# Attention with a feed-forward layer on one core: the products' moving columns are read from two halves in turn

## The chip, the core and the metric

The kernel runs on one core of a Trainium2 chip. The metric is the device time of one execution in microseconds (us). Before the change it was 906.98 us, the median of three runs that lay between 906.57 and 907.24 us.

## What is computed

The reference computes attention and, on its output, a feed-forward layer. Attention has 8 batches, 8 heads, 576 tokens and a head size of 64; it is causal, each token sees the 128 newest tokens, and a slope per head is added to the scores:

```
scores = scale * q @ k.T ; bias by distance ; keep 0 <= rel < 128 ; softmax ; @ v
x   = attention output as (4608 tokens, 512)
h   = max(x @ w_in, 0)            # w_in: 512 x 2048
out = (h * h) @ w_out             # w_out: 2048 x 512
```

All of it is float32. The tokens are independent of one another in the feed-forward layer, so their order inside a block of columns is free as long as the output is put back.

## The kernel before, in words

The 4608 tokens are nine chunks of 512. Activations lie with features on the 128 partitions and tokens along the free dimension, so in every product of the feed-forward layer the weights are stationary (128 by 128) and the tokens are the moving columns. The output is written transposed (512 features by 4608 tokens), and the host turns it back with `.T` at the end of `kernel` (line 1542).

**Float32r in three products.** TensorE's float32r type keeps fewer bits than float32. Each operand is therefore split into a high part and a low part, and a block is the sum of three products: high by high, low weight by high, high weight by low. Every such product is one weight load and one matmul.

**Four places issue float32r products.** `gemm1` (line 244) is the first layer for chunks 0 and 1: 12 matmuls of 512 columns for each of the 16 feature blocks f of a chunk. `product` (line 344) is the first layer for chunks 2 to 8; there a pair of feature blocks, two halves of the reduction and two halves of the chunk's tokens make a 2 by 2 problem that is done in seven products, not eight, each of six matmuls of 256 columns (7 chunks x 8 pairs x 7 x 6 = 2352). `part` (line 518) is the second layer for chunks 0 to 7: 16 f x 4 blocks x 3 matmuls of 512 columns a chunk. `third` (line 432) is the second layer of the last chunk, again in seven products: 8 pairs x 2 x 7 x 3 = 336 matmuls of 256 columns. The attention products (lines 601, 650, 714, 873, 886, 918) and the transposes (955, 958) are plain float32 and small.

**Where the weights lie.** Converted weights are kept as `w[f]` with shape `[128, 2, 512, 2]`: the last index is low or high part, so `block` (line 227) hands out weights in which one column lies two words behind the last. For a quarter of the first layer's feature blocks (`APART`, line 41: f = 0, 4, 8, 12, blocks 0 and 1) two columns' pairs are laid alternately, so there one column lies four words behind the last. For the seven products, `operand` (line 307) hands out pieces 0, 3 and 5 of the tile `flow` with a step of two words and the other four with neighbouring columns. In `third`, M1, M2 and M4 take `w` with a step of two words, the rest the tile `second` with neighbouring columns.

**Moving operands.** `x[c, p]` (tile `xu`, shape `[128, 2, 512]`), `tees`, `hh`, `hl`, `h2`, `keep` and `turned` all hold a product's 256 or 512 columns as neighbouring words; each matmul reads them from first to last.

**Order of the work.** A planner (`Plan.run`) takes steps with written costs, due times and hand-tuned nudges, simulates the queues and issues the instructions in the order that it finds; that order is fixed when the program is built. The planner's costs of PE steps (such as 0.7 for a block of `part`) are numbers in the code. From chunk 2 on, a visit of about 4 us with attention work comes between the products every 24 us.

## Time and profile before

| | |
|---|---|
| median of three runs | 906.98 us (906.57 to 907.24) |
| the profiled execution | its time is given by its span alone, 905.9 us from the first to the last instruction |
| instructions | 23570 |
| matmuls on PE | 8700, each with its own weight load |
| granted TensorE clock | 1.000 over the whole span |

The profile shows one execution. Engines: PE is TensorE's matmul, PEld its weight load, DVE is VectorE, ACT is ScalarE, POOL is GpSimd, SP issues DMAs. Matmuls are pipelined: a matmul's listed duration reaches well into the next one, so the pace is read from one start to the next, or from the chain of work, whose pieces follow one another without overlap.

### The profile page before, as it was taken

To read this page: it belongs to the slowest core of one execution; us is meant where nothing else is said; L and a number is where in the kernel's file an instruction comes from. 1 tells how busy PE (TensorE), PEld (TensorE's weight loads), DVE (VectorE), ACT (ScalarE), POOL (GpSimd) and SP (SyncE) were. 2 spreads that over 40 slices of the span, in tenths; PEclk is the share of its full clock that TensorE was granted. 3 is DMA by queue.
4 is the path that set the end of the run, shared out by engine and by line. 5 is a ranking of instruction groups with operands and counts; after the bars stand their busy time and mean duration, and the time that the engine had idled before them with its cause. 6 is when DMAs were issued, how large, how long until landed. Compare 5 with 4: busy or idle time off the path is not lost.

```text
span 905.9 us, 23570 instructions
## 1 busy us (share of the span) xinstructions
PE 899.1 (99%) x8700; PEld 807.1 (89%) x8700; DVE 629.8 (70%) x1695; ACT 482.0 (53%) x1361; POOL 319.4 (35%) x403
## 2 busy tenths in 40 slices
PE   9999999999999999999999999999999999999998
PEld 6788888888899999999999999999999999989998
DVE  6998882677775677666766786676766565566675
ACT  7899663665654555444544555445545454444341
POOL 4222334665522333234333433233322222234341
DMA  9976326768888888788887788888887777669962
GB/s 347 404 279 213 88 62 200 244 225 265 300 273 285 286 269 261 261 281 271 284 270 265 259 269 272 294 265 273 267 301 241 232 238 225 209 204 341 301 226 94
DMA packets 142324, 229.77 MB, mean 254 GB/s; under 512 B 15744, under 2 KB 50176, under 8 KB 142208
## 3 DMA queue, kind: packets, MB, share of 16 engines
q1 hardware_dynamic: 141920, 227.87, 75.4%
q8 instruction: 68, 1.11, 0.5%
q10 hardware_dynamic: 288, 0.39, 0.1%
q14 instruction: 48, 0.39, 0.1%
HBM read 178.91 MB, written 49.28 MB: 252 GB/s over the span
## 4 chain that ended last, share of the span: by engine, by line
PE 95%; DMA 4%; ACT 0%; POOL 0%; issue 0%; DVE 0%; SPq 0%; POOLq 0%; DVEq 0%
PE acc L518 40%; PE chain L344 18%; PE rest L344 13%; PE g L244 10%; PE s L873 5%; PE acc L432 2%; PE g L886 2%; DMA raw<-in_dram 2%; PE s L432 1%; PE s L886 1%; DMA wide<-in_dram 1%; PE at L650 1%; DMA qk<-in_dram 1%; PE s L714 0%; PE chain L432 0%; PE rest L432 0%
## 5 line engine op out<-in xcount | busy, mean ns | idle before, releaser
L518 PE MATMUL acc<-hh,w 128*128 128x512 f32 x1024 | 361.8, 398 | 0.0
L518 PEld LDWEIGHTS acc<-hh,w 128*128 128x128 f32 x1024 | 200.4, 196 | 35.9 <-issue 5.5
L518 PE MATMUL acc<-hl,w 128*128 128x512 f32 x512 | 202.2, 395 | 0.0
L638 POOL TENSOR_SCALAR_AFFINE_SELECT pp<-pp 128x512 f32<-128x512 f32 x128 | 99.3, 785 | 169.2 <-DMA pp<-way 122.6
L571 POOL TENSOR_TENSOR t<-t,nm 128x512 f32<-128x512 f32 x64 | 67.8, 1062 | 250.4 <-DVE nm L567 191.9
L344 PEld LDWEIGHTS rest<-xu,flow 128*128 128x128 f32 x1008 | 142.5, 191 | 11.7
L344 PE MATMUL chain<-tees,flow 128*128 128x256 f32 x1008 | 147.4, 282 | 0.0
L344 PE MATMUL rest<-xu,flow 128*128 128x256 f32 x1008 | 146.8, 281 | 0.0
L364 ACT COPY four<-chain 128x256 f32<-128x256 f32 x56 | 20.9, 374 | 233.6 <-PE chain L344 233.6
L349 DVE TENSOR_TENSOR four<-four,rest 128x256 f32<-128x256 f32 x112 | 47.2, 421 | 124.8 <-PE rest L344 122.1
L344 PEld LDWEIGHTS chain<-tees,flow 128*128 128x128 f32 x1008 | 132.2, 191 | 0.0
L518 PEld LDWEIGHTS acc<-hl,w 128*128 128x128 f32 x512 | 100.3, 196 | 11.1
L559 ACT ACTIVATE t<-t,nm 128x128 f32<-128x128 f32 x256 | 100.3, 394 | 8.8 <-DVE nm L552 8.2
L244 PE MATMUL g<-xu,w 128*128 128x512 f32 x384 | 95.2, 396 | 0.0
L244 PEld LDWEIGHTS g<-xu,w 128*128 128x128 f32 x384 | 76.5, 209 | 12.8 <-issue 0.3
L552 DVE CUSTOM_DVE_ANT_0 t<-t,cst 128x128 f32<-128x128 f32 x256 | 62.8, 300 | 1.7
L262 DVE TENSOR_TENSOR hl<-r,hh 128x512 fp32r<-128x512 f32 x32 | 29.2, 913 | 45.0 <-ACT hh L260 45.0
L873 PE MATMUL s<-pp,v 64*64 64x128 f32 (+1 forms) x1792 | 52.3, 248 | 0.2
L344 PEld LDWEIGHTS chain<-xu,flow 128*128 128x128 f32 x336 | 48.2, 196 | 4.1 <-ACT four L364 0.5
L786 DVE COPY_PREDICATED t<-cst,s 64x256 f32<-64x256 int32 x100 | 44.4, 444 | 8.1 <-PE s L873 4.5
L344 PE MATMUL chain<-xu,flow 128*128 128x256 f32 x336 | 49.7, 284 | 0.0
L559 ACT ACTIVATION_READ_ACCUMULATOR t<-t,nm 128x1 f32 x256 | 48.3, 189 | 0.0
(159 smaller groups left out, 1378.0 us busy)
## 6 DMA issues: line engine op xcount, KB each, us to landing
flow<-ws SPq DMA_DIRECT2D x392, 256.0 KB, 5.1
raw<-in_dram SPq DMA_DIRECT2D x32, 512.0 KB, 8.8
way<-pp SPq DMA_DIRECT2D x256, 64.0 KB, 2.3
pp<-way SPq DMA_DIRECT2D x64, 256.0 KB, 2.7
qk<-in_dram SPq DMA_DIRECT2D x32, 320.0 KB, 5.7
v<-in_dram SPq DMA_DIRECT2D x32, 320.0 KB, 5.7
qk<-in_dram SPq DMA_DIRECT2D x38, 256.0 KB, 5.5
out_dram<-o SPq DMA_DIRECT2D x34, 256.0 KB, 3.2
```

What stands on the lines that cost most here:

```text
L244: nc.tensor.matmul(g, w, xs[cc][:, part], start=i == 0, stop=i == 11)
L262: nc.vector.tensor_tensor(hl, r, hh.bitcast(F32), op=ALU.subtract)
L344: self.latest = self.nc.tensor.matmul(to, w, x, start=start and k == 0, stop=k == 5, skip_group_check=True)
L349: add = lambda to, x: nc.vector.tensor_tensor(to, to, x, op=ALU.add)
L432: self.nc.tensor.matmul(self.total[u][name], w, x, start=j == k == 0 and name in ("M1", "M3", "M5", "M2"), stop=j == NF // 2 - 1 and k == ...
L518: self.latest = self.nc.tensor.matmul(self.acc[m], w, h, start=(f == 0 and i == 0), stop=(f == NF - 1 and i == 2))
L552: self.nc.vector.tensor_tensor_reduce(self.t[:, m], self.t[:, m], self.K.nrel(2 * self.p + m // 2), -0.125, BIG, ALU.add, ALU.min, self.nm ...
L559: return self.nc.scalar.activation(self.t[:, m], self.t[:, m], AF.Exp, bias=nm[:, 4 + m : 5 + m], scale=-1.0, accum_out=nm[:, m : m + 1],)
L571: self.nc.gpsimd.tensor_tensor(*(x.rearrange("p (j i) c -> p j i c", j=2) for x in (self.t, self.t)), self.rec.unsqueeze(3).to_broadcast([ ...
L638: nc.gpsimd.affine_select(to, self.own, pattern=[[-32 * sign, 4], [0, 4], [-sign, 32]], compare_op=op, fill=0.0, base=0, channel_multiplie ...
L786: nc.vector.copy_predicated(d, mask.unsqueeze(1).to_broadcast([64, 2, 2, 64]), e)
L873: yield self.nc.tensor.matmul(to, w, x, start=first and n < 2, stop=not first, skip_group_check=True)
```

## The change

Each of the four places that issue float32r products reads its moving columns through a helper, `turns`. It leaves the tile where it is and reads columns 0, h, 1, h+1, 2, h+2 and so on, where h is half the number of columns (256 of 512, or 128 of 256). The product's output is still written to neighbouring words, so the tokens of a chunk come out in another order. Both layers turn the order once. For chunks 0 and 1 both turn the whole chunk; for chunks 2 to 7 the first layer turns each half of 256 columns and the second the whole; for chunk 8 both turn each half. The host undoes this by indexing the columns of the output before it transposes it. No other instruction, tile, DMA, planner cost or due time is edited.

```
+def turns(x):
+    return x.rearrange("p (h c) -> p c h", h=2)

 gemm1:
-                nc.tensor.matmul(g, w, xs[cc][:, part], start=i == 0, stop=i == 11)
+                nc.tensor.matmul(g, w, turns(xs[cc][:, part]), start=i == 0, stop=i == 11)
 product:
-            self.latest = self.nc.tensor.matmul(to, w, x, start=start and k == 0, stop=k == 5, skip_group_check=True)
+            self.latest = self.nc.tensor.matmul(to, w, turns(x), start=start and k == 0, stop=k == 5, skip_group_check=True)
 third:
-                self.total[u][name], w, x, start=...
+                self.total[u][name], w, turns(x), start=...
 part:
-            self.latest = self.nc.tensor.matmul(self.acc[m], w, h, start=(f == 0 and i == 0), stop=(f == NF - 1 and i == 2))
+            self.latest = self.nc.tensor.matmul(self.acc[m], w, turns(h), start=(f == 0 and i == 0), stop=(f == NF - 1 and i == 2))

+def _order():
+    turn = lambda n: np.arange(n).reshape(2, n // 2).T.reshape(-1)
+    whole, half = turn(512), np.concatenate([turn(256), 256 + turn(256)])
+    at = np.empty(B * S, int)
+    for c in range(NCH):
+        one, two = whole if c < 2 else half, half if c == NCH - 1 else whole
+        at[512 * c + one[two]] = 512 * c + np.arange(512)
+    return at

 kernel:
-    return np.ascontiguousarray(r.results[0]["out_0_dram"].T)
+    return np.ascontiguousarray(r.results[0]["out_0_dram"][:, _order()].T)
```

## Rows read from the trace of the kernel before

**Rows 1.** The page, part 1: busy time, share of the span and instructions of each engine.
```profile
PE 899.1 (99%) x8700; PEld 807.1 (89%) x8700; DVE 629.8 (70%) x1695; ACT 482.0 (53%) x1361; POOL 319.4 (35%) x403
```

**Rows 2.** The chain that ended last, shares of the span by line.
```profile
by line: PE acc L518 40.0%; PE chain L344 17.7%; PE rest L344 13.1%; PE g L244 9.6%; PE s L873 4.8%; PE acc L432 2.5%; PE g L886 2.4%; DMA raw<-in_dram 2.0%; PE s L432 1.3%; PE s L886 1.2%; DMA wide<-in_dram 1.0%; PE at L650 0.8%; DMA qk<-i
```

**Rows 3.** Waits: all of PE's, PEld's longest, then other engines': us, times, longest.
```profile
PE g L173 <- DVE zero L166: 1.3, 1, 1.3
PE acc L601 <- DVE xu L614: 1.1, 3, 0.6
PE s L714 <- ACT raw L215: 0.8, 1, 0.8
...
PEld acc L518 <- issue: 5.5, 32, 0.2
...
ACT four L364 <- PE chain L344: 233.6, 56, 5.3
...
DVE four L349 <- PE rest L344: 122.1, 100, 5.0
```

**Rows 4.** Chain pieces in order of time: start us, length us, engine, tile, line, matmuls.
```profile
48.49 2.80 PE g L244 x12
51.29 2.80 PE acc L518 x12
...
118.22 2.80 PE g L244 x12
121.02 2.80 PE acc L518 x12
...
174.45 2.76 PE g L244 x12
```

**Rows 5.** Busy time by windows: window, us, engines (instructions), clock, DMA share, GB/s.
```profile
50.00:100.00 50.00, 50.00 (x353) 42.12 (x352) 44.00 (x97) 44.42 (x91) 13.53 (x20) 1.00 0.58 196
100.00:150.00 50.00, 50.00 (x305) 41.86 (x305) 34.33 (x76) 27.70 (x66) 18.90 (x23) 1.00 0.32 87
400.00:450.00 50.00, 50.00 (x548) 45.63 (x550) 37.08 (x105) 25.60 (x77) 18.60 (x25) 1.00 0.85 284
```

**Rows 6.** Timeline of PE, five bf16 warming matmuls of 768 columns in all, and the next.
```profile
27.71 0.50 PE L173 MATMUL g<-zero 128*128 128x128 bf16 x5
28.04 0.28 PE L955 MATMUL at<-cst,tw 128*128 128x128 f32 x1
```

**Rows 7.** Timeline of PE around 411 us (start us, us): two products and the next.
```profile
411.14 0.88 PE L344 MATMUL rest<-xu,flow 128*128 128x256 f32 x6
411.86 0.88 PE L344 MATMUL chain<-tees,flow 128*128 128x256 f32 x6
412.57 0.40 PE L518 MATMUL acc<-hh,w 128*128 128x512 f32 x1
```

**Rows 8.** Groups of matmuls and of small weight loads by form: busy us, mean ns.
```profile
L518 PE MATMUL acc<-hh,w 128*128 128x512 f32 x1024 | 361.8, 398 | 0.0
L518 PE MATMUL acc<-hl,w 128*128 128x512 f32 x512 | 202.2, 395 | 0.0
L244 PE MATMUL g<-xu,w 128*128 128x512 f32 x384 | 95.2, 396 | 0.0
...
L873 PEld LDWEIGHTS s<-pp,v 64*64 64x64 f32 x1792 | 40.7, 134 | 5.1 <-issue 1.1 <-POOLq L890 0.4 <-POOL both L291 0.4
```

**Rows 9.** Weight loads of single lines: duration ns min/median/max; the last 59.3 to 60.5 us.
```profile
L432 PEld LDWEIGHTS s<-xu,second x72: 186/188/193, 835.7 to 896.7; 128*128 128x128 f32 x72
L432 PEld LDWEIGHTS acc<-xu,w x48: 193/197/203, 840.6 to 899.2; 128*128 128x128 f32 x48
...
L244 PEld LDWEIGHTS g<-xu,w x6: 308/310/311, 59.3 to 60.5; 128*128 128x128 f32 x6
```

**Rows 10.** Timeline of PE, first and seventh matmul of feature block 4 in `gemm1`.
```profile
59.53 2.72 PE L244 MATMUL g<-xu,w 128*128 128x512 f32 x11
...
60.94 1.31 PE L244 MATMUL g<-xu,w 128*128 128x512 f32 x5
```

**Rows 11.** Timeline of PE after a visit: the first two matmuls of line 518.
```profile
403.97 0.51 PE L518 MATMUL acc<-hh,w 128*128 128x512 f32 x1
404.31 0.40 PE L518 MATMUL acc<-hl,w 128*128 128x512 f32 x1
```

## The prediction

> **What bounds the kernel now.** I read the busy shares first. PE is busy for 899.1 of 905.9 us, while DVE stands at 70% [rows 1]. A busy PE can still be one that is held up inside, so the chain of work came next: the float32r lines 518, 344 and 244 alone are 80.4% of the span, and line 432 adds 3.8% [rows 2]. The waits say that nobody feeds PE late: its three waits sum to 3.2 us, while ACT and DVE wait for PE by the hundred microseconds [rows 3]. So the time is the number of float32r matmuls times their pace, and a change in that pace comes out in the total almost one for one.

> The pace: twelve matmuls of 512 columns take 2.80 us, 233.3 ns each, or 2.76 us, 230 ns each, in one stretch [rows 4]. For 256 columns the chain gives 17.7% + 13.1% of 905.9 us = 279.0 us over 2352 matmuls, 118.6 ns each [rows 2]; six in a row take 0.71 to 0.72 us, the same [rows 7]. [...]

> **The change part by part.** It removes no instruction and adds none; the order on each queue is the planner's, whose costs are untouched, and the DMAs are the same. The host's indexing is outside the device's time. What changes is the address of each moving column. With the halves taken in turn, the even columns are the neighbouring words of the first half, the odd ones those of the second. No row of this trace shows a product read in that way, so I bound it.

> Products of 512 columns: 1024 + 512 + 384 = 1920 [rows 8]. The chain gives them (40.0% + 9.6%) of 905.9 us, 449.3 us or 234.0 ns each [rows 2]. In 32 places [rows 3] the first one after a visit takes 340 ns, some 107 more than the others [rows 11]; that is 3.4 us which stay, so the pace in the stream is 232.2 ns. With two readers at 0.84 ns for their own column the stream would run at 0.42 a column: 512 x 0.42 + 3.9 = 219 ns; the bf16 row gives 215.5. I take 217 and a gain of 15.2 ns: 29.2 us. Of these, 2 x 4 x 6 = 48 in line 244 have loads with a step of four words, and there the loads set the pace already: six matmuls in 60.94 − 59.53 = 1.41 us, 235 ns, beside 310 − 80 = 230 ns of reading [rows 9, 10]. They gain nothing, which takes off 0.7 us. Sum 28.5 us; bounds 25 (219) and 31 (215.5).

> Products of 256 columns: 2352 + 336 = 2688. By columns alone they would fall from 118.6 to 256 x 0.42 + 3.9 = 111.4. But the next load must be read meanwhile, and the row above says pace = reading + 5 ns where the load is longer. Neighbouring weights: 108 + 5 = 113 ns. Weights with a step of two words: 117 + 5 = 122, more than they take now, so I give those nothing. Four of seven products have neighbouring weights, 1344 + 192 = 1536: (118.6 − 113) x 1536 = 8.6 us. Bounds: 0, if the loads already set the pace of all, and 9.9 x 2688 = 26.6 us, if they set none (108.7).

> [...]

> What is late next: in the window from 50 to 100 us ACT is busy for 44.4 and DVE for 44.0 of 50 us [rows 5], so a PE that is 6% faster there would meet weights and hidden blocks that aren't ready. The cover is thin for that window alone; I take 1 us back, with 0 and 3 us (the window's whole gain) as ends. In the later windows DVE has a quarter of its time free and the DMA share of 0.85 would rise to about 0.88.

> Sum: −28.5 − 8.6 + 1 = −36 us, 4% of 905.9. The median of the runs lies 1.1 us above the profiled span, and the same is assumed after: 907 − 36 = 871 us.

> **The rivals.** (1) *Slower: one group held at a time.* If both columns of a step come out of one fetch by one reader, then after the change each column needs a fetch of its own. The loads show what this does: from a step of two words to four, a column doubles. It decides from the point where two columns in a row lie in different groups, which is every column here. A column of a product would go from 0.448 to 0.896: +229 ns for 512 columns, +115 for 256, 1920 x 0.229 + 2688 x 0.115 = 749 us, a time of about 1656 us. At the 1.80 of a whole fetch for each column it would be 3170. For it speaks the load row at 310 ns, the only strided one of that kind; against it, that a product's two columns cost what a load's step of two costs. [...] (2) *No change.* If two groups are held at once but by one fetcher, there are as many fetches as before, 128 for 512 columns, and the pace stays: 907 us. [...] (3) *All of it.* If the weights with a step of two words don't hold their products either, the bounds are reached: 907 − 31 − 26.6 = 849 us. (4) *Less of it.* If the loads already set the pace of all products of 256 columns, 907 − 28.5 + 1 = 880.

> **How the numbers follow.** Two readers, gain as summed, 871 us: 0.45. All of it, 849: 0.14. Less of it, 880: 0.14. No change, 907: 0.07. One group at a time, 1656 or more: 0.20. About 0.2% (1.8 us) is what a measurement of this kernel can tell from no change. So faster 0.73, same 0.07, slower 0.20. The range goes from just under 849 to 909 and takes in every case but the slow one: 847 to 909. The forecast's own range is 860 to 882.

> **What would show it.** In the chain, pieces of twelve on lines 518 and 244 should fall from 2.80 to about 2.60 us, while the first six of line 244 at a step of four words stay at 235 ns each. On line 344 products with neighbouring weights should take 0.68 us for six, the others 0.72. Loads should keep their durations. PE should still be busy for 98% or more, with a few waits for ACT or DVE before 100 us. The forecast is wrong if pieces of twelve are at 5.5 us or more (one group at a time), or still at 2.80, or if the 256-column products gain as much a column as the long ones.

## The result, and the profile after the change

The kernel after the change takes 884.7 us (median of four runs, 883.4 to 886.12) beside 906.84 us (906.57 to 907.24) before: a ratio of 0.9754, interval 0.9739 to 0.9768. The forecast was 871 us. The gain has the forecast's sign, but is 22.1 us where 36 were forecast. The profiled execution took 883.4 us with a span of 881.7 us, 24.2 us less than the span before. Lines behind the new helper stand five lower now, so that 244, 344, 432 and 518 are 249, 349, 437 and 523, and `convert`'s 215 to 223 are 220 to 228.

The busy shares of the kernel after, in the form of [rows 1]:

```profile
PE 863.8 (98%) x8700; PEld 801.0 (91%) x8700; DVE 643.3 (73%) x1695; ACT 488.1 (55%) x1361; POOL 329.2 (37%) x403
```

PE lost 35.3 us of busy time, nearly as many as the forecast wanted from the whole. But DVE gained 13.5 us and ACT 6.1, though their instructions are the same. The chain by engine, first before and then after the change, and the chain of the kernel after by line, against [rows 2]:

```profile
PE 95%; DMA 4%; ACT 0%; POOL 0%; issue 0%; DVE 0%; SPq 0%; POOLq 0%; DVEq 0%
```

```profile
PE 74%; DMA 13%; DVE 6%; issue 2%; ACT 2%; POOL 1%; SPq 1%; DVEq 0%; POOLq 0%; ACTq 0%
PE acc L523 30%; PE chain L349 16%; PE rest L349 12%; PE s L878 5%; PE g L249 4%; DMA flow<-ws 3%; DMA raw<-in_dram 3%; PE acc L437 2%; PE g L891 2%; DMA pp<-way 2%; DVE w L228 2%; DVE raw L224 1%; DMA way<-pp 1%; POOL pp L643 1%; PE s L437 1%
```

The chain now runs outside PE for a quarter of the span, where before it was on PE for 95%. Its pieces in order of time show the first long stretch of this (start, length, work), against [rows 4]:

```profile
85.54 1.55 ACT raw L220
...
97.44 1.54 DVE raw L224
99.00 1.63 ACT w L226
100.66 1.64 DVE w L228
102.91 1.56 DVE raw L224
...
144.30 3.00 PE g L249 x12
147.30 2.59 PE acc L523 x12
149.89 2.59 PE g L249 x12
152.48 2.59 PE acc L523 x12
```

Between 41 and 141 us it runs for the most part over the conversion of weights (`convert`, lines 220 to 228), over other work of DVE and over DMAs; then over products again, of which twelve take 2.59 us, 215.8 ns each, not 2.80. Later it leaves PE again, mainly for DMAs, at 169, 286, 396 and 423 us. That the chain runs elsewhere doesn't say that PE stands still there; the windows do. They are, for the kernel after (columns as in [rows 5]):

```profile
50.00:100.00 50.00, 46.52 (x339) 39.59 (x339) 45.91 (x84) 48.13 (x85) 17.50 (x17) 1.00 0.58 193
100.00:150.00 50.00, 45.60 (x295) 39.69 (x294) 40.38 (x89) 31.68 (x76) 20.35 (x21) 1.00 0.27 71
400.00:450.00 50.00, 48.73 (x525) 45.84 (x524) 39.48 (x114) 27.08 (x86) 18.12 (x25) 1.00 0.85 293
```

PE was busy for all of each window before. Now 7.9 of the 100 us from 50 to 150 are idle, 3.5 of them before 100 us and 4.4 behind it, while ACT is at 48.1 of the first 50 us and DVE at 45.9. PE's longest waits between 45 and 166 us (who, for whom; us, times, longest), where it waited for nothing before the change:

```profile
PE at L655 <- POOL pp L643: 3.2, 4, 1.2
PE g L249 <- ACT r L258: 2.0, 4, 1.0
PE at L655 <- ACT t L772: 1.4, 1, 1.4
PE s L719 <- ACT r L263: 0.8, 1, 0.8
```

None of them is for a converted weight. They are for other instructions of ACT and POOL, which now come later. The conversions themselves, in the view of groups (busy us, mean ns, idle before), first before and then after:

```profile
L223 DVE TENSOR_TENSOR w<-raw,w 128x1024 fp32r<-128x1024 f32 x16 | 21.2, 1331 | 0.2
L219 DVE SCALAR_TENSOR_TENSOR raw<-raw 128x1024 int32<-128x1024 int32 x16 | 20.4, 1281 | 0.4
L215 ACT ACTIVATE raw<-raw 128x1024 f32<-128x1024 f32 x16 | 18.1, 1170 | 0.0
L221 ACT CAST w<-raw 128x1024 fp32r<-128x1024 f32 x13 | 14.8, 1144 | 0.3 <-DVE raw L219 0.2
```

```profile
L228 DVE TENSOR_TENSOR w<-raw,w 128x1024 fp32r<-128x1024 f32 x16 | 25.8, 1620 | 0.5 <-ACT w L226 0.3
L224 DVE SCALAR_TENSOR_TENSOR raw<-raw 128x1024 int32<-128x1024 int32 x16 | 25.5, 1606 | 0.4
L220 ACT ACTIVATE raw<-raw 128x1024 f32<-128x1024 f32 x16 | 22.4, 1473 | 0.0
L226 ACT CAST w<-raw 128x1024 fp32r<-128x1024 f32 x13 | 20.3, 1578 | 2.5 <-DVE raw L224 2.4
```

The same instructions on the same data take 22 to 38% longer, 19.5 us more over these four groups. (A fifth step of `convert`, DVE's shift in line 222, goes from 684 to 827 ns.) All of them read and write every second word (`raw` and `w` hold pairs), on engines that the change doesn't touch; the cast of `hh` from the neighbouring words of `r` is as before (622 ns, 620 before). So the first question for the experiments is whether the order in which PE reads can slow other engines, and the second whether the two readers are the right picture of the gain.

Products of 256 columns, the timeline of PE around 411 us after the change, against [rows 7] (start, us):

```profile
411.06 0.88 PE L349 MATMUL chain<-xu,flow 128*128 128x256 f32 x6
411.77 0.39 PE L523 MATMUL acc<-hh,w 128*128 128x512 f32 x1
...
413.08 0.83 PE L349 MATMUL rest<-xu,flow 128*128 128x256 f32 x6
413.75 0.83 PE L349 MATMUL chain<-tees,flow 128*128 128x256 f32 x6
414.42 0.39 PE L523 MATMUL acc<-hh,w 128*128 128x512 f32 x1
```

The first product has weights with a step of two words and takes 0.71 us for six as before; the other two have neighbouring weights and take 0.67 us, 112 ns each.

### The profile page after: what moved, and what is told of

It reads as the page before. It is cut to its first block, busy times and chain, and to the rows that moved or that the text cites. A ratio compares the mean times of both kernels' runs of the same rounds, so it can differ in the third digit from the quotient of the medians.

```text
span 881.7 us, 23570 instructions
## 1 busy us (share of the span) xinstructions
PE 863.8 (98%) x8700; PEld 801.0 (91%) x8700; DVE 643.3 (73%) x1695; ACT 488.1 (55%) x1361; POOL 329.2 (37%) x403
## 4 chain that ended last, share of the span: by engine, by line
PE 74%; DMA 13%; DVE 6%; issue 2%; ACT 2%; POOL 1%; SPq 1%; DVEq 0%; POOLq 0%; ACTq 0%
PE acc L523 30%; PE chain L349 16%; PE rest L349 12%; PE s L878 5%; PE g L249 4%; DMA flow<-ws 3%; DMA raw<-in_dram 3%; PE acc L437 2%; PE g L891 2%; DMA pp<-way 2%; DVE w L228 2%; DVE raw L224 1%; DMA way<-pp 1%; POOL pp L643 1%; PE s L437 1%
## 5 line engine op out<-in xcount | busy, mean ns | idle before, releaser
L523 PE MATMUL acc<-hh,w 128*128 128x512 f32 x1024 | 347.7, 384 | 0.0
L523 PE MATMUL acc<-hl,w 128*128 128x512 f32 x512 | 194.3, 379 | 0.1
L643 POOL TENSOR_SCALAR_AFFINE_SELECT pp<-pp 128x512 f32<-128x512 f32 x128 | 106.9, 843 | 178.8 <-DMA pp<-way 110.7
L349 PEld LDWEIGHTS rest<-xu,flow 128*128 128x128 f32 x1008 | 140.2, 194 | 6.8 <-DVE four L354 0.5
L349 PE MATMUL chain<-tees,flow 128*128 128x256 f32 x1008 | 142.7, 278 | 0.0
L349 PE MATMUL rest<-xu,flow 128*128 128x256 f32 x1008 | 142.3, 277 | 0.1
L349 PEld LDWEIGHTS chain<-tees,flow 128*128 128x128 f32 x1008 | 128.6, 194 | 0.0
L249 PE MATMUL g<-xu,w 128*128 128x512 f32 x384 | 90.8, 386 | 2.0 <-ACT r L258 2.0
L557 DVE CUSTOM_DVE_ANT_0 t<-t,cst 128x128 f32<-128x128 f32 x256 | 64.6, 309 | 1.7
L791 DVE COPY_PREDICATED t<-cst,s 64x256 f32<-64x256 int32 x100 | 44.4, 444 | 10.2 <-PE s L878 6.5
L267 DVE TENSOR_TENSOR hl<-r,hh 128x512 fp32r<-128x512 f32 x32 | 26.7, 835 | 31.4 <-ACT hh L265 31.3
```

Source lines behind the costliest of these rows:

```text
L249: nc.tensor.matmul(g, w, turns(xs[cc][:, part]), start=i == 0, stop=i == 11)
L267: nc.vector.tensor_tensor(hl, r, hh.bitcast(F32), op=ALU.subtract)
L349: self.latest = self.nc.tensor.matmul(to, w, turns(x), start=start and k == 0, stop=k == 5, skip_group_check=True)
L523: self.latest = self.nc.tensor.matmul(self.acc[m], w, turns(h), start=(f == 0 and i == 0), stop=(f == NF - 1 and i == 2))
L557: self.nc.vector.tensor_tensor_reduce(self.t[:, m], self.t[:, m], self.K.nrel(2 * self.p + m // 2), -0.125, BIG, ALU.add, ALU.min, self.nm ...
L643: nc.gpsimd.affine_select(to, self.own, pattern=[[-32 * sign, 4], [0, 4], [-sign, 32]], compare_op=op, fill=0.0, base=0, channel_multiplie ...
```

## The experiments

In all of them `turns` takes a second argument, a pattern, and each layer has a list with one pattern for each chunk (`ONE` for the first, `TWO` for the second); the host's order follows from the lists. "Partners" are two columns that are read one right after the other; in the change they lie 256 words apart (128 in a product of 256 columns).

```
+WAYS = {"plain": ("p c -> p c", {}),
+        "halves": ("p (h c) -> p c h", dict(h=2)),            # the change
+        "quarters": ("p (h c) -> p c h", dict(h=4)),
+        "pairs": ("p (h c b) -> p c h b", dict(h=2, b=2)),
+        "second": ("p (c h) -> p h c", dict(h=2)),            # every second column
+        "near16": ("p (b h c) -> p b c h", dict(h=2, c=16)),  # partners 16 words apart
+        ...
+def turns(x, way):
+    if way == "plain":
+        return x
+    pattern, sizes = WAYS[way]
+    return x.rearrange(pattern, **sizes)
```

### Chunk 0 as before, and chunk 0 with near partners

The conversions run beside chunk 0's products, so chunk 0 alone was edited, first back to plain reading, then to partners 16 words apart:

```
e1: ONE = ["plain"] + ["halves"] * 8;   TWO = ["plain"] + ["halves"] * 8
e3: ONE = ["near16"] + ["halves"] * 8;  TWO = ["near16"] + ["halves"] * 8
```

> Chunk 0 reads its columns in plain order in both layers, all other chunks in turned halves. Theory A (the turned reading itself slows the weight conversions of ACT and DVE, which step over every second word, and PE then waits for them): the conversions return to 1.17 and 1.14 us on ACT and 1.28 and 1.33 us on DVE (with the change 1.47, 1.58, 1.61, 1.62), the products of chunk 0 take 233 ns again, PE reaches the first product of chunk 1 after its attention visit near 158 us instead of 163 us, and the time is about 880 us, less than with the change everywhere. Rival B (the conversions are merely late because PE became faster, and turned reading still gains a little in chunk 0): without it the time is 885 to 891 us.

> As with the change, but chunk 0 takes halves in turn inside blocks of 32 columns, so that partners lie 16 words apart instead of 256. If theory A holds and what disturbs the conversions is that two groups are fetched for each pair of columns, nothing changes: products 216 ns, conversions 1.47 to 1.62 us, 885 us. If it is the distance (two places of memory that collide with a third), the conversions come back towards 1.15 to 1.33 us and the time falls to between 872 and 880 us.

Measured: chunk 0 plain 879.01 us (877.32 to 879.31), ratio to before 0.9678 (0.9662 to 0.9695); its conversions are back at 1163, 1142, 1270 and 1292 ns (in the order ACT raw, ACT cast, DVE raw, DVE w of the table below), with chunk 0's products at 233 ns. Undoing the change in one chunk of nine makes the kernel 5.7 us faster. Chunk 0 near: 873.69 us (872.16 to 875.68), ratio 0.9627 (0.961 to 0.9644): here chunk 0's products take 216 ns and the conversions their old time all the same. Its groups and its first window:

```profile
L245 DVE TENSOR_TENSOR w<-raw,w 128x1024 fp32r<-128x1024 f32 x16 | 20.5, 1286 | 0.2
L241 DVE SCALAR_TENSOR_TENSOR raw<-raw 128x1024 int32<-128x1024 int32 x16 | 20.2, 1269 | 0.4
L237 ACT ACTIVATE raw<-raw 128x1024 f32<-128x1024 f32 x16 | 18.3, 1176 | 0.0
L243 ACT CAST w<-raw 128x1024 fp32r<-128x1024 f32 x13 | 15.2, 1181 | 0.3 <-DVE raw L241 0.2
```

```profile
50.00:100.00 50.00, 50.00 (x366) 44.76 (x365) 46.74 (x101) 47.34 (x98) 16.34 (x21) 1.00 0.61 202
```

PE is never idle between 50 and 100 us, with 366 matmuls against 339 after the change and 353 before. What slows the conversions is thus the place of the partners, and neither the faster pace of PE nor the turning in itself. A common point in the order of work tells how much it cost: the first product of the second layer after the visit at about 160 us, which stands behind the same work in all kernels. In the timeline of PE it is, after the change and then with chunk 0 near:

```profile
164.95 0.49 PE L523 MATMUL acc<-hh,w 128*128 128x512 f32 x1
```

```profile
155.18 0.49 PE L540 MATMUL acc<-hh,w 128*128 128x512 f32 x1
```

Before the change:

```profile
160.30 0.51 PE L518 MATMUL acc<-hh,w 128*128 128x512 f32 x1
```

So the change is 4.6 us late there, the near version 5.1 us early. From there to the end of the span the change takes 716.8 us, the near version 717.6, the kernel before 745.6: the whole difference between the first two lies ahead of this point.

### Which orders are fast

The second layer alone was turned, with another pattern in each chunk, everything else plain:

```
e2: ONE = ["plain"] * 9
    TWO = ["plain", "plain", "halves", "quarters", "pairs", "second", "near16", "near4", "plain"]
```

> All products in plain order, as before, except those of the second layer with 512 columns, which read in another order in each chunk: chunks 0 and 1 plain, 2 halves in turn, 3 quarters in turn, 4 pairs of columns from two halves in turn, 5 every second column and then the others, 6 halves in turn inside blocks of 32 columns (partner 16 words away), 7 the same in blocks of 8 (4 words away). Theory of two readers (even and odd columns, each holding one group of four words): plain 230 to 234 ns, halves, blocks of 32 and blocks of 8 216 ns, and quarters, pairs and every second column slow, 400 to 470 ns, since each reader meets a new group in every column. Rival of one reader that holds two groups: pairs also 216, quarters slow, every second column as plain. Rival of the place (columns from far apart never wait): quarters and pairs 216, blocks of 8 as plain.

Measured: 970.95 us, with 512-column products of 216 ns for halves and for partners 16 and 4 words apart, and medians of 280 ns for quarters, 331 for pairs and 453 for every second column, beside 231 to 233 for plain. Pieces of the chain, six products each, in chunks 2 (halves), 3 (quarters), 4 (pairs), 5 (every second column) and 6 (near16):

```profile
265.71 1.30 PE acc L540 x6
...
440.23 1.72 PE acc L540 x6
...
512.56 1.98 PE acc L540 x6
...
632.53 2.72 PE acc L540 x6
...
748.26 1.30 PE acc L540 x6
```

The picture of two readers, one for each column of a step, agrees with halves and near partners: they take 216 ns, and each reader's own columns would be neighbouring words there. With every second column each of two readers would step by four words, and the 453 ns come near the price that the slow rival had worked out (233 + 229 = 462). But quarters and pairs (280 and 331 ns) came out well below the 400 to 470 ns that two readers with one group each give, so the picture of two readers isn't complete: if it holds, a reader keeps more than it allows. How much stays open. The readers and their groups remain the author's inference from the loads and these durations; no run shows them.

Quarters were also put into chunk 0 of the full change:

```
e4: ONE = ["quarters"] + ["halves"] * 8;  TWO = ["quarters"] + ["halves"] * 8
```

> As with the change, but chunk 0 reads four quarters in turn. Two readers: its 384 products take 400 to 470 ns instead of 216, so the time rises by 70 to 100 us, to between 955 and 985 us; this separates the pace of PE from its way of reading. Theory A (way of reading): the conversions stay slow, at least 1.4 us each on ACT and DVE, although PE is slow and nothing is late. Rival B (pace): with a slow PE they take what they took before the change, 1.14 to 1.33 us.

Measured: 897.37 us, chunk 0's products at 284 ns, conversions at 1167, 1148, 1264 and 1260 ns. The 400 to 470 ns of two readers and the slow conversions of theory A both failed to come: quarters have partners 128 words apart, and don't disturb. Rival B, by which the pace of PE does it, got the conversions right here, but the run with near partners (216 ns, nothing disturbed) rules it out.

### Which distances disturb

Chunk 0 again, with partners 128, 64 and 32 words apart in both layers, and one with a distance that is large but not a multiple of 64: the first layer of chunk 0 at 16, its second layer with 8 words left empty between the halves of `hh` and `hl`, so that partners lie 264 words apart.

```
e7:  ONE[0] = TWO[0] = "near128"
e9:  ONE[0] = TWO[0] = "near64"
e10: ONE[0] = TWO[0] = "near32"
e12: ONE[0] = "near16"; TWO[0] = "halves", and
-        hh = self.hp.tile([128, 512], F32R, name="hh")
-        hl = self.hp.tile([128, 512], F32R, name="hl")
+        hh, hl = (self.hp.tile([128, 528], F32R, name=name) for name in ("hh", "hl"))
+        if c == 0:
+            hh, hl = (x.rearrange("p (h c) -> p h c", h=2)[:, :, 0:256] for x in (hh, hl))
...
```

> As with the change, but chunk 0 takes halves in turn inside blocks of 256 columns, partners 128 words apart instead of 256. Products 216 ns. If it is the distance of 256 words alone that disturbs the weight conversions, these take what they took before (ACT 1.15 to 1.2 us, DVE 1.25 to 1.35 us) and the time is 872 to 876 us. If any long distance disturbs them, they take 1.45 us or more and the time is 882 to 887 us.

> As with the change, but chunk 0's partners lie 64 words apart (blocks of 128 columns). Distances of 256 and 128 words disturb the weight conversions (about 1.5 to 1.6 us on ACT), 16 does not (1.17). Theory D (places that are a multiple of some period apart collide, and 16 words is less than the period): at 64 either disturbed, 1.45 us or more and 879 to 886 us, which puts the period at 64 words or below, or as before, 1.15 to 1.2 us and 871 to 876 us, which puts it above 64. Rival E (the longer the distance, the more it disturbs): values between, 1.25 to 1.4 us.

> As above with partners 32 words apart (blocks of 64 columns). Theory D: either 1.45 us or more (period 32 words or below) or 1.15 to 1.2 us; and never disturbed if 64 is undisturbed. Rival E: less than at 64, between 1.2 and 1.3 us. Products 216 ns in either case.

> As with the change, but in chunk 0 the first layer's partners lie 16 words apart, and the second layer's hidden blocks are stored with a gap of 8 words between their halves, so that partners lie 264 words apart, far but no multiple of 64. Theory D (a multiple of 64 words collides): the weight conversions are as before, ACT 1.15 to 1.2 us, DVE 1.25 to 1.35 us, and the time is 870 to 877 us. Rival F (any distance of 64 words or more disturbs): the second layer's half of chunk 0 still disturbs them, 1.28 to 1.45 us on ACT, and the time is 877 to 882 us. Products 216 ns either way.

Measured, with the other runs for comparison (mean ns of the four conversions; kernels with one run show that run):

| chunk 0's partners | ACT raw | ACT cast | DVE raw | DVE w | time, us |
|---|---|---|---|---|---|
| before (plain everywhere) | 1170 | 1144 | 1281 | 1331 | 906.84 |
| plain | 1163 | 1142 | 1270 | 1292 | 879.01 |
| 16 words apart | 1176 | 1181 | 1269 | 1286 | 873.69 |
| 32 words | 1193 | 1188 | 1270 | 1290 | 872.19 |
| 64 words | 1473 | 1582 | 1587 | 1637 | 883.08 |
| 128 words | 1495 | 1541 | 1582 | 1575 | 881.25 |
| 256 words (the change) | 1473 | 1578 | 1606 | 1620 | 884.7 |
| 16, second layer 264 | 1186 | 1178 | 1274 | 1289 | 872.9 |

One row of each of the runs with 64, 32 and 16/264 words, in that order:

```profile
L238 ACT ACTIVATE raw<-raw 128x1024 f32<-128x1024 f32 x16 | 22.6, 1473 | 0.0
```

```profile
L238 ACT ACTIVATE raw<-raw 128x1024 f32<-128x1024 f32 x16 | 18.5, 1193 | 0.0
```

```profile
L238 ACT ACTIVATE raw<-raw 128x1024 f32<-128x1024 f32 x16 | 18.4, 1186 | 0.2 <-DMA raw<-in_dram 0.2
```

There is nothing gradual: at 64, 128 and 256 words all four conversions are slow and the kernel takes 881 to 885 us; at 16, 32 and 264 none is, and it takes 872 to 874. That 256 words alone disturb fell with the run at 128, that any large distance does fell with 264. Multiples of 64 words (256 bytes) fit all of these distances. Others, such as 192 or 320 words, weren't run, so the period is an inference from the distances run, and what makes it isn't shown. In the run with 264 words the distance was changed in half of chunk 0's products, so it shows that these don't disturb, not what the first layer would do with a gap.

This counts only if the second layer's products disturb at 256 words by themselves, and no run turned them alone in chunk 0. The traces settle it, since some casts ran wholly beside products of the second layer. One after the change, and one with 264 words:

```profile
51.83 1.56 ACT L226 CAST w<-raw 128x1024 fp32r<-128x1024 f32 x1
```

```profile
104.65 1.18 ACT L244 CAST w<-raw 128x1024 fp32r<-128x1024 f32 x1
```

After the change there are three such casts on ACT, 1.56 to 1.78 us, and two wholly beside products of the first layer, 1.68 and 1.79; with 264 words four beside the second layer took 1.16 to 1.23. So either layer disturbs at 256 words.

### The weights of the 256-column products

To test what holds the 256-column products, all seven pieces were stored so that their weights have a step of two words. Against the kernel after, the instructions that write these pieces have that step too:

```
e6:
-        both = self.hole(2 * j, f"both{j}", [128, 2, 4, 2, 128])
-        lo, hi = both[:, :, :, 0], both[:, :, :, 1]
+        both = self.hole(2 * j, f"both{j}", [128, 2, 4, 128, 2])
+        lo, hi = both[..., 0], both[..., 1]
...
-            w = self.flow[n % 2][i].rearrange("p (k t d) -> p k t d", k=2, t=2)
-            return [(w[:, k, 0], w[:, k, 1]) for k in range(2)]
+            w = self.flow[n % 2][i].rearrange("p (k d t) -> p k d t", k=2, t=2)
+            return [(w[:, k, :, 0], w[:, k, :, 1]) for k in range(2)]
```

> With the change, and the four products of seven whose weights lay as neighbouring words now get them with a step of two words, as the other three have them. Theory (a load with a step of two words sets the pace of a 256-column product): rows of six that took 0.67 us take 0.71 to 0.72 us, 1344 products rise from 112 to 119 or 120 ns, 9 to 11 us in all, so the time is 893 to 897 us. Rival (the three slower products are slow for another reason, their accumulator or their place in the order): the four stay at 112 ns and the time stays at 885 us, within 3 us.

Measured: 894.06 us, 9.4 more than with the change. The same two products as above:

```profile
413.07 0.87 PE L366 MATMUL rest<-xu,flow 128*128 128x256 f32 x6
413.78 0.89 PE L366 MATMUL chain<-tees,flow 128*128 128x256 f32 x6
414.50 0.39 PE L540 MATMUL acc<-hh,w 128*128 128x512 f32 x1
```

They take 0.71 and 0.72 us where they took 0.67: the load's step sets the pace of a turned product of 256 columns. ACT's casts of the pieces (`both`, 512 words), which run beside chunk 1's turned products, went from 615 to 914 ns with the step of two; how much of that the step alone costs wasn't run. The other half of the question is what these products are worth, so only those of 512 columns were turned:

```
e8: ONE = ["halves"] * 2 + ["plain"] * 7;  TWO = ["halves"] * 8 + ["plain"]
```

> Turned halves only in the products of 512 columns (both layers of chunks 0 and 1, the second layer up to chunk 7); the products of 256 columns read in plain order and stay at 119 ns. The 256-column products' share of the change is then 10 to 12 us, less what they give back in waits: 892 to 897 us. The start is as with the change, 163 us at the first product after chunk 0. If the 256-column products give back all they gain, 885 us.

Measured: 891.64 us (890.36 to 893.58), ratio 0.9833 (0.9818 to 0.9849). Turning the products of 256 columns as well is worth 6.9 us of the 22.1.

### Near partners everywhere

```
e5:  ONE = TWO = ["near16"] * 9
e11: ONE = TWO = ["near4"] * 9
```

> Every float32r product takes halves in turn inside blocks of 32 columns, so partners lie 16 words apart everywhere. Theory C (only partners 256 words apart disturb others; near partners read as fast): products as in the kernel with near partners in chunk 0 alone, 216 and 112 to 120 ns, and the time is 866 to 874 us, at most what that kernel took (873.7). If near partners cost something in the 256-column products or beside their weight loads, these rise above 112 to 120 ns and the time lies above 876 us.

> Every float32r product takes halves in turn inside blocks of 8 columns, partners 4 words apart: the two readers work in neighbouring groups. If what counts for the pace is only that each reader uses all four words of its group, products take 216 and 112 to 120 ns as with 16 words; theory D then expects undisturbed conversions and 867 to 872 us. If neighbouring groups collide, the conversions or the pace suffer, and the time is above 875 us.

Measured: 869.35 us (867.05 to 870.06), ratio 0.9581 (0.9564 to 0.9598), for 16 words, and 873.41 us (870.58 to 876.47), ratio 0.964 (0.9609 to 0.9671), for 4. Both have products of 216 and 112 ns and undisturbed conversions (ACT's cast 1166 and 1151 ns, DVE's `w` 1285 and 1290). With 4 words the time lies between the 867 to 872 us and the above 875 that were expected of the two theories; why it is 4 us behind 16 words isn't settled. The one with 16 words is the fastest kernel here, 15.4 us ahead of the change. Its busy shares:

```profile
PE 857.5 (99%) x8700; PEld 796.8 (92%) x8700; DVE 633.3 (73%) x1695; ACT 479.1 (55%) x1361; POOL 321.4 (37%) x403
```

## Why the prediction was right in part

**PE's pace comes out in the time.** Right as long as the pace was the only thing that changed. In the kernel with 16 words everywhere, products that are 7 and 6% faster shorten the span by 38.4 us.

**Products of 512 columns.** Forecast 217 ns, measured 215.8 (2.59 us for twelve): (232.2 − 215.8) x 1872 = 30.7 us where 28.5 were forecast. The forecast's 0.448 ns a column, its double of 0.896 for two columns and its 3.9 ns a matmul are estimates from the chain's figures, (233.3 − 118.6) / 256 and 233.3 − 512 x 0.448. The 215.5 that it takes from the bf16 row for 512 columns, and the 108.7 for 256, with the bounds of 31 and 26.6 us and the rival at 849, were the author's estimate, and no run shows what they rest on. In their place the runs showed 215.8 ns for turned products of 512 columns and, for 256, 112 with neighbouring weights and 118 to 120 with a step of two words; the fastest kernel took 869.35 us. The 48 matmuls with loads at a step of four words gained nothing, as forecast; their loads took 309 to 345 ns and they some 240.

**Products of 256 columns.** Forecast 113 ns with neighbouring weights and no gain with a step of two; measured 112 and 118 to 120. That is (118.6 − 112) x 1536 = 10.1 us instead of 8.6, and the run with all weights at a step of two words shows that the load is the reason.

**What is late next: the step that failed.** It gave back 1 us, at most 3, because the cover on ACT and DVE is thin between 50 and 100 us. Of 30.7 + 10.1 = 40.8 us won in the stream, 24.2 reached the span, so 16.6 were given back. At the visit at 160 us, 447 products of 512 columns lie behind, 30 of them with loads at a step of four; the other 417 fell from 2.80 to 2.59 us for twelve, 17.5 ns each, worth 7.3 us. The change was 4.6 us late there instead, a loss of 11.9 us. The place was right only in part, as more of PE's idle time lies behind 100 us (4.4) than before it (3.5), and the cause was another. The step reckoned with DVE and ACT at their old durations and with a PE that outruns them. What came was a PE whose reading order made the conversions 22 to 38% longer, in a stretch where ACT and DVE had little time free. POOL's masking of `pp` became longer too, from 827 to 1210 ns on average before 165 us (950 with chunk 0 near), and 3.2 of PE's 7.9 idle us end on it; whether PE's reading or DVE's longer instructions stretched it isn't shown. With chunk 0 near, the same step at the old durations cost 7.3 − 5.1 = 2.2 us, inside the forecast's 0 to 3; and that kernel's 873.7 us lie 3 us from the 871 forecast, in part by luck: of its 40.8 us, not 37.1 as forecast, 7.7 were given back, not 1.

The other 4.7 us (16.6 − 11.9) were lost later. With chunk 0 near they are still there; with 16 words everywhere only 40.8 − 38.4 = 2.4 us are lost in all. The forecast put nothing for this stretch. PE's waits behind 166 us, after the change and then with 16 words everywhere, where before the change there are none:

```profile
PE s L878 <- POOL pp L643: 3.0, 4, 1.1
```

```profile
PE s L895 <- POOL pp L660: 2.0, 2, 1.1
```

Four waits for POOL's `pp` are 3.0 of the 4.7 us; what the rest is wasn't settled.

**The rivals.** One group at a time did not come for halves, although columns that follow each other lie far apart: 216 ns, not 462. Other orders came nearer to it: quarters took 280 ns, pairs 331 and every second column 453. No change and all of it are excluded by 2.59 us for twelve and by 0.71 us for six. Less of it (880) lies nearest to the 884.7 measured, but by chance: its mechanism, loads that hold all products of 256 columns, is refuted by the 112 ns. None of the rivals had PE slow another engine. The range of 847 to 909 held the time; the forecast's own range, 860 to 882, missed it by 2.7 us.

## What to carry to other kernels

A float32r product of 512 columns took 233 ns here where it read neighbouring words from first to last, and 216 where it read two blocks in turn, each block's words being neighbours. Choose blocks 16 or 32 words apart (ACT's cast beside them took 1181 and 1188 ns on average), not 64, 128 or 256 (1541 to 1582), and give products of 256 columns weights that are neighbouring words (112 ns, against 118 to 120 with a step of two). When an edit changes only how one engine reads, compare the mean durations of the other engines' groups first: the loss stood there, not on PE.

## What was not expected of the hardware

ACT and DVE instructions that read and write every second word became 18 to 38% longer (the cast went from 1144 to between 1541 and 1582 ns) when PE's partners lay 64, 128 or 256 words apart, and not at 16, 32 or 264 (1178 to 1188). These means mix two kinds: ACT's line 220 took 1.15 us at 21 us, ahead of the first float32r product, and 1.70 and 1.81 where it ran beside products of the first layer alone. Four blocks in turn 128 words apart didn't do it, at a slower pace of PE (284 ns; the cast took 1148), and why not stays open. Nothing but PE's reading order in chunk 0 differs between the 1181 and the 1578 ns of the cast on ACT; how the reading comes to lengthen it isn't shown.
